# First feature block of two tiles ahead, x2 and x3 requested later, Gelu table preloaded: the start of a fused attention and GLU kernel

## The chip, the cores and the metric

The kernel runs on one core of a Trainium2 chip. The metric is the device time of one execution, in microseconds. Engines are called PE (matrix multiply), VectorE (DVE in the profile), ACT (ScalarE), POOL and SP, which issues the DMAs. Where this text says "trace", it means one profiled execution; a time is a median of several executions, unless said otherwise.

## The reference

```
xn = layernorm(x)                              # x: 1 x 2048 x 512, bf16
qkv = xn @ wqkv                                # 512 x 1536; 32 heads of 16
attention over 8 positions, 2 apart, its own the last;   s = attn @ wo
g = silu((gelu(xn @ w_gate) * (xn @ w_up)) @ w_down)    # inner width 1792
out = x + s * g
```

The 2048 rows are 16 tiles of 128, and four row blocks of 512. Feature blocks are the four groups of 128 of the 512 features; a matmul contracts over one of them.

## The kernel before

The start, cut to what the change touches. `x_sb[:, t]` is tile t; `wqkv_sb[:, k]` is weight block k. All DMAs are issued by SP in program order. The scheduler is off: each engine runs its instructions in the order written.

```python
    for i in range(2):
        for t in (2 * i, 2 * i + 1):
            load_x(t)
        for k in (2 * i, 2 * i + 1):
            nc.sync.dma_start(out=wqkv_sb[:, k, :], in_=A_wqkv[k * P : (k + 1) * P, :])
    load_x(TPQ, TPQ)                    # tiles 4 to 7; then w_gate, w_up, the rest of x
    ...
    first_stats(0); first_moments(0)    # VectorE statistics, then ACT square root
    first_stats(1); first_rstd(0); first_moments(1)
    normalize(0)                        # VectorE, 512 columns
    transpose(0)                        # four PE transposes, one ACT copy
    first_rstd(1); normalize(1)
    warm_up(4, P)
    transpose(1, parts=2, copy=nc.vector.tensor_copy)   # two copies
    for t in (2, 3): first_stats(t); first_moments(t)
    for t in (2, 3): first_rstd(t); normalize(t)
    for dk in range(NC):                # 4 blocks of 12 matmuls on tiles 0 and 1
        for n, (fo, ps) in enumerate(pairs):
            ...two matmuls 128 x 256...
            if dk == 2 and n in (2, 5):
                transpose(2 + (n == 5), copy=nc.vector.tensor_copy)
    ...
    for t in range(TPQ, 2 * TPQ): moments(t)            # statistics of tiles 4 to 7
    ...projections of tiles 2 and 3 ("second half"), then the GLU of row block 0...
```

The softmax here doesn't subtract the row's maximum and nothing guards it: scores larger than these inputs give would overflow.

## Time and profile before

| | kernel before |
|---|---|
| time, three executions | 229.1 us (229.09 to 229.49) |
| span of the trace | 227.4 us |
| PE busy | 98% |
| first matmul that counts | 6.55 us |
| second-half projections start | 12.45 us |
| second up-projection starts | 20.93 us |

PE sets the end. From 6.55 us to the tail it has almost no gap, so what matters is when PE starts and whether something then makes it wait. The three last rows are used as marks; they are starts in PE's timeline, which lists instructions by start and length. The profile's lines for this are in the prediction.

### The profile page before, as it was taken

How to read it: one execution, taken by the hardware profiler on the slowest of the kernel's cores; microseconds unless marked ns; L12 is line 12 of the kernel's file. 1: busy time of each engine (PE TensorE's matmuls, PEld its weight loads, DVE VectorE, ACT ScalarE, POOL GpSimd, SP SyncE). 2: the span in 40 equal slices, each digit the busy share in tenths (PEclk: the TensorE clock that was granted, in tenths of full speed). 3: DMA queues.
4: the chain of work that ended last, by engine and by line, in shares of the span. 5: the costliest groups of instructions: out<-in, count | busy, mean ns of one | idle time of the engine just before them, and what ended most of it. 6: DMA issues, size and time to landing. Idle time of an engine off the chain costs nothing.

```text
span 227.4 us, 3595 instructions
## 1 busy us (share of the span) xinstructions
PE 222.3 (98%) x1326; PEld 107.1 (47%) x1326; DVE 151.8 (67%) x278; ACT 132.2 (58%) x209; POOL 25.0 (11%) x67
## 2 busy tenths in 40 slices
PE   8999999999999999999999999999999999999993
PEld 4785444444444444444444444444444444444453
DVE  4696981899995588969904759924934348971434
ACT  4279769777531676766751466767763356756210
POOL 1027901000040000333700000000000000000000
PEclk9999999999999999999999999999999999999998
DMA  6999499941039911100219921100217950000011
GB/s 206 349 395 384 127 201 142 321 109 67 28 83 202 223 25 25 29 10 0 92 33 206 214 71 29 26 18 0 81 26 151 197 140 0 0 0 22 12 37 56
DMA packets 30130, 24.64 MB, mean 108 GB/s; under 512 B 10784, under 2 KB 29600, under 8 KB 30112
## 3 DMA queue, kind: packets, MB, share of 16 engines
q1 hardware_dynamic: 30112, 24.41, 44.3%
q8 instruction: 10, 0.16, 0.3%
q14 instruction: 8, 0.07, 0.1%
HBM read 18.74 MB, written 4.34 MB: 102 GB/s over the span
## 4 chain that ended last, share of the span: by engine, by line
PE 95%; DVE 1%; ACT 1%; DMA 1%; issue 0%; DVEq 0%
PE y_ps L443 21%; PE u_ps L249 21%; PE g_ps L249 21%; PE qkv_ps L249 16%; PE s_ps L459 6%; PE L_ps L338 3%; PE o_ps L406 3%; PE qk_ps L554 2%; DMA x_sb<-in_A_x_dram 1%; PE v_ps L554 1%; ACT L431 1%; DVE stats L182 1%; PE tr L214 1%; PE den_ps L358 0%; ACT ge L431 0%; ACT vst L273 0%
## 5 line engine op out<-in xcount | busy, mean ns | idle before, releaser
L249 PE MATMUL u_ps<-xnT,wu_sb 128*128 128x512 bf16 x224 | 57.5, 379 | 0.0
L249 PE MATMUL g_ps<-xnT,wg_sb 128*128 128x512 bf16 x224 | 57.5, 379 | 0.0
L443 PE MATMUL y_ps<-wd_sb,h 128*128 128x512 bf16 (+1 forms) x238 | 49.9, 367 | 0.0
L435 DVE TENSOR_TENSOR h<-ge,u 128x512 bf16<-128x512 bf16 x56 | 23.8, 425 | 30.7 <-ACT u L433 29.0
L433 ACT ACTIVATE u<-u_ps 128x512 bf16<-128x512 f32 x56 | 33.5, 598 | 16.4 <-PE u_ps L249 16.4
L431 ACT ACTIVATE ge<-g_ps 128x512 bf16<-128x512 f32 x56 | 33.5, 598 | 16.2 <-PE g_ps L249 16.0
L320 DVE TENSOR_TENSOR pk<-q_sb,k_sb 128x1024 bf16<-128x1024 bf16 (+1 forms) x56 | 38.9, 762 | 4.6 <-ACT k_sb L273 4.6
L392 DVE TENSOR_TENSOR pv<-E,v_arr 128x1024 bf16<-128x1024 bf16 (+1 forms) x48 | 39.8, 863 | 0.2 <-issue 0.2
L249 PE MATMUL qkv_ps<-xnT,wqkv_sb 128*128 128x512 bf16 (+1 forms) x192 | 37.0, 352 | 0.0
L443 PEld LDWEIGHTS <-h 128*128 128x128 bf16 x238 | 23.0, 98 | 25.9 <-issue 1.3
L249 PEld LDWEIGHTS <-wu_sb 128*128 128x128 bf16 x224 | 21.9, 98 | 26.6 <-issue 0.3
L249 PEld LDWEIGHTS <-wg_sb 128*128 128x128 bf16 x224 | 21.7, 98 | 26.3 <-issue 0.8
L451 ACT ACTIVATE sl<-y_ps 128x512 bf16<-128x512 f32 (+1 forms) x17 | 9.7, 572 | 32.6 <-PE y_ps L443 32.6
L249 PEld LDWEIGHTS <-wqkv_sb 128*128 128x128 bf16 x192 | 18.8, 98 | 17.5
L467 DVE TENSOR_TENSOR m<-s_ps,sl 128x512 bf16<-128x512 f32 (+1 forms) x17 | 11.1, 655 | 17.0 <-PE s_ps L459 17.0
L418 DVE TENSOR_TENSOR oT<-o_ps,rb 128x1024 bf16<-128x1024 f32 x8 | 9.4, 1220 | 13.8 <-DMA rb<-rs_d 13.8
L199 POOL TENSOR_TENSOR rstd<-rstd,mhalf 128x1 f32<-128x1 f32 x12 | 8.0, 663 | 69.9 <-DVE rstd L196 69.9
L459 PE MATMUL s_ps<-wo_sb,oT 128*128 128x512 bf16 (+1 forms) x68 | 14.8, 366 | 0.0
L273 ACT ACTIVATE vst<-qkv_ps 128x512 bf16<-128x512 f32 x14 | 8.4, 597 | 3.7 <-PE qkv_ps L249 3.7
L273 ACT ACTIVATE k_sb<-qkv_ps 128x512 bf16<-128x512 f32 x14 | 8.4, 601 | 3.2 <-PE qkv_ps L249 3.2
L273 ACT ACTIVATE q_sb<-qkv_ps 128x512 bf16<-128x512 f32 x14 | 8.3, 603 | 3.0 <-PE qkv_ps L249 3.0
L459 PEld LDWEIGHTS <-oT 128*128 128x128 bf16 x68 | 6.7, 98 | 7.2
(57 smaller groups left out, 131.4 us busy)
## 6 DMA issues: line engine op xcount, KB each, us to landing
v_arr<-vT SPq DMA_DIRECT2D x16, 520.0 KB, 8.5
vT<-vst SPq DMA_DIRECT2D x8, 256.0 KB, 2.2
out_dram<-o_t SPq DMA_DIRECT2D x15, 128.0 KB, 3.4
wg_sb<-in_B_w_gate_dram SPq DMA_DIRECT2D x2, 896.0 KB, 10.1
wu_sb<-in_B_w_up_dram SPq DMA_DIRECT2D x2, 896.0 KB, 11.0
wd_sb<-in_B_w_down_dram SPq DMA_DIRECT2D x1, 1792.0 KB, 11.5
wqkv_sb<-in_A_wqkv_dram SPq DMA_DIRECT2D x4, 384.0 KB, 4.9
x_sb<-in_A_x_dram SPq DMA_DIRECT2D x3, 512.0 KB, 10.5
```

The costliest lines, as they stand in the source:

```text
L249: nc.tensor.matmul(ps, lhsT=w[:, dk, lo : lo + P], rhs=xnT[j][:, dk, i0 : i0 + n], start=(dk == 0), stop=(dk == NC - 1),)
L273: nc.scalar.activation(out=dst, in_=ps, func=AF.Copy)
L320: nc.vector.tensor_tensor(out=st[j]["pk"][w][:, c0 : c0 + n, :], in0=st[j]["q"][:, c0 : c0 + n, :], in1=k_sb[j][:, c0 : c0 + n, off : off ...
L392: nc.vector.tensor_tensor(out=pv[:, d : d + n, :], in0=st[j]["E"][:, wh, :].unsqueeze(1).to_broadcast([P, n, TQ]), in1=st[j]["va"][:, 4 * ...
L418: nc.vector.tensor_tensor(out=oT[:, g : g + 2, :], in0=st[j]["o"][:, g : g + 2, :], in1=st[j]["rb"][:].unsqueeze(1).to_broadcast([P, 2, TQ ...
L431: nc.scalar.activation(out=ge[:], in_=g_ps[:], func=AF.Gelu_apprx_tanh)
L433: nc.scalar.activation(out=u[:], in_=u_ps[:], func=AF.Copy)
L435: nc.vector.tensor_tensor(out=h[:], in0=ge[:], in1=u[:], op=ALU.mult)
L443: nc.tensor.matmul(y[:], lhsT=st[j][fc][:, tt * P : (tt + 1) * P], rhs=wd_sb[:, fc, cols], start=(fc == 0), stop=(fc == NF - 1),)
L451: nc.scalar.activation(out=sl[:], in_=y[:], func=AF.Silu)
L459: nc.tensor.matmul(s[:], lhsT=st[j]["oT"][:, g, tt * P : (tt + 1) * P], rhs=wo_sb[:, g, cols], start=(g == 0), stop=(g == NC - 1),)
L467: nc.vector.tensor_tensor(out=m[:], in0=s[:], in1=sl[:], op=ALU.mult)
```

## The change

The intent: PE needs only the first feature block of tiles 0 and 1 to begin. So that block alone is normalized, transposed and copied first, and the other three follow behind the first six matmuls. Weight block 2, for which PE waited at 9.17, is requested ahead of x2 and x3. The Gelu table is loaded while ACT has nothing else to do.

```diff
-    for i in range(2):
-        for t in (2 * i, 2 * i + 1):
-            load_x(t)
-        for k in (2 * i, 2 * i + 1): ...
+    for t in (0, 1): load_x(t)
+    for k in range(NC - 1): load_wqkv(k)
+    for t in (2, 3): load_x(t)
+    load_wqkv(NC - 1)
... normalize() and transpose() take a list of feature blocks ...
-    normalize(0)
-    transpose(0)
+    normalize(0, [0])
+    transpose(0, [0])
+    warm_up(2, P)
     first_rstd(1)
-    normalize(1)
-    warm_up(4, P)
-    transpose(1, parts=2, copy=nc.vector.tensor_copy)
-    ...statistics and normalization of tiles 2 and 3...
+    normalize(1, [0])
+    transpose(1, [0])
+    normalize(0, rest)
+    normalize(1, rest)
     for dk in range(NC): ...
+            if dk == 0 and n == 2:
+                transpose(0, rest)
+                transpose(1, rest, nc.vector.tensor_copy)
+                for t in (2, 3): first_stats(t); first_moments(t)
+                nc.scalar.preload_act_table(AF.Gelu_apprx_tanh)
+                for t in (2, 3): first_rstd(t); normalize(t)
```

More of the change, by code (lines that the diff above doesn't have):

```diff
@@ L96, in load_w, with load_wqkv @@
         )
-    for i in range(2):
-        for t in (2 * i, 2 * i + 1):
-            load_x(t)
-        for k in (2 * i, 2 * i + 1):
-            nc.sync.dma_start(out=wqkv_sb[:, k, :], in_=A_wqkv[k * P : (k + 1) * P, :])
+    def load_wqkv(k):
+        nc.sync.dma_start(out=wqkv_sb[:, k, :], in_=A_wqkv[k * P : (k + 1) * P, :])
+    for t in (0, 1):
+        load_x(t)
+    for k in range(NC - 1):
+        load_wqkv(k)
+    for t in (2, 3):
+        load_x(t)
+    load_wqkv(NC - 1)
     load_x(TPQ, TPQ)
@@ L201, with normalize, transpose @@
     xns = {}
-    def normalize(t):
-        xn = xns[t] = xnp.tile([P, D], BF16, name="xn")
+    def normalize(t, cs=range(NC)):
+        if 0 in cs:
+            xns[t] = xnp.tile([P, D], BF16, name="xn")
+        cols = slice(cs[0] * P, (cs[-1] + 1) * P)
         nc.vector.tensor_scalar(
-            out=xn[:], in0=x_sb[:, t, :], scalar1=mv[:, t, 0:1], scalar2=rstd[:, t, :],
+            out=xns[t][:, cols], in0=x_sb[:, t, cols],
+            scalar1=mv[:, t, 0:1], scalar2=rstd[:, t, :],
             op0=ALU.subtract, op1=ALU.mult,
         )
-    def transpose(t, parts=1, copy=None):
-        xn = xns[t]
-        tr = mm.tile([P, NC * P], BF16, name="tr", tag="mm")
-        for c in range(NC):
-            nc.tensor.transpose(tr[:, c * P : (c + 1) * P], xn[:, c * P : (c + 1) * P], ident[:])
+    trs = {}
+    def transpose(t, cs=range(NC), copy=None):
+        if 0 in cs:
+            trs[t] = mm.tile([P, NC * P], BF16, name="tr", tag="mm")
+        tr = trs[t]
+        for c in cs:
+            nc.tensor.transpose(
+                tr[:, c * P : (c + 1) * P], xns[t][:, c * P : (c + 1) * P], ident[:]
+            )
         j, i = divmod(t, TPQ)
-        if i == 0:
+        if j not in xnT:
             xnT[j] = xtp.tile([P, NC, TQ], BF16, name="xnT")
-        dst = xnT[j][:, :, i * P : (i + 1) * P]
-        src = tr[:].rearrange("p (c n) -> p c n", c=NC)
-        for k in range(parts):
-            c = slice(k * NC // parts, (k + 1) * NC // parts)
-            if copy is None or k % 2:
-                nc.scalar.activation(out=dst[:, c], in_=src[:, c], func=AF.Copy)
-            else:
-                copy(out=dst[:, c], in_=src[:, c])
+        c = slice(cs[0], cs[-1] + 1)
+        dst = xnT[j][:, c, i * P : (i + 1) * P]
+        src = tr[:].rearrange("p (c n) -> p c n", c=NC)[:, c]
+        if copy is None:
+            nc.scalar.activation(out=dst, in_=src, func=AF.Copy)
+        else:
+            copy(out=dst, in_=src)
     def warm_up(n, cols):
@@ L533 @@
     warm_up(4, P)
+    rest = range(1, NC)
     first_stats(0)
@@ L538 @@
     first_moments(1)
-    normalize(0)
-    transpose(0)
+    normalize(0, [0])
+    transpose(0, [0])
+    warm_up(2, P)
     first_rstd(1)
-    normalize(1)
-    warm_up(4, P)
-    transpose(1, parts=2, copy=nc.vector.tensor_copy)
-    for t in (2, 3):
-        first_stats(t)
-        first_moments(t)
-    for t in (2, 3):
-        first_rstd(t)
-        normalize(t)
+    normalize(1, [0])
+    transpose(1, [0])
+    normalize(0, rest)
+    normalize(1, rest)
     for dk in range(NC):
@@ L560 @@
                 )
+            if dk == 0 and n == 2:
+                transpose(0, rest)
+                transpose(1, rest, nc.vector.tensor_copy)
+                for t in (2, 3):
+                    first_stats(t)
+                    first_moments(t)
+                nc.scalar.preload_act_table(AF.Gelu_apprx_tanh)
+                for t in (2, 3):
+                    first_rstd(t)
+                    normalize(t)
             if dk == 2 and n in (2, 5):
```

## The prediction

> **What bounds the kernel now.** I read the page first, for shares, then the chain that ended last, to see where TensorE stops being the end-setter.
>
> ```profile
> PE 222.3 (98%) x1326; PEld 107.1 (47%) x1326; DVE 151.8 (67%) x278; ACT 132.2 (58%) x209; POOL 25.0 (11%) x67
> ...
> PE 95%; DVE 1%; ACT 1%; DMA 1%; issue 0%; DVEq 0%
> ```
>
> PE is busy 98% of the span and is 95% of the chain, so outside PE's idle time only PE work can be saved. The edit touches only the start and one table load, so I followed the chain in order of time through the first 25 us.
>
> ```profile
> 0.80 2.12 DMA x_sb<-in_A_x_dram
> ...
> 5.69 0.40 PE tr L214 x4
> ...
> 6.12 0.30 DVE xnT L225
> 6.42 0.14 issue
> 6.55 0.60 PE v_ps L554 x4
> ...
> 17.89 0.60 ACT vst L273
> 18.48 0.49 ACT xnT L223
> ...
> 18.99 1.28 ACT L431
> ...
> 20.28 0.61 ACT ge L431
> ...
> 20.93 1.02 PE u_ps L249 x4
> ```
>
> Columns are start, length, what. Until 6.55 the chain is x's landing, statistics, normalization, transpose and copy; from 6.55 it is PE, with one detour through ACT at 17.89 to 20.93 which contains a table load of 1.28 us. The whole head that the edit can attack is thus what lies before 6.55, plus PE's small gaps. PE's gaps come from its timeline (start, length, engine, line, operation; consecutive equal ones merged):
>
> ```profile
> 7.86 0.60 PE L554 MATMUL v_ps<-xnT,wqkv_sb 128*128 128x256 bf16 x4
> 8.30 1.04 PE L554 MATMUL qk_ps<-xnT,wqkv_sb 128*128 128x256 bf16 x8
> 9.37 0.61 PE L554 MATMUL v_ps<-xnT,wqkv_sb 128*128 128x256 bf16 x4
> 9.81 0.38 PE L554 MATMUL qk_ps<-xnT,wqkv_sb 128*128 128x256 bf16 x2
> 10.03 0.39 PE L214 MATMUL tr<-ident,xn 128*128 128x128 bf16 x4
> 10.26 0.82 PE L554 MATMUL qk_ps<-xnT,wqkv_sb 128*128 128x256 bf16 x6
> ```
>
> A block dk of 12 matmuls takes 1.31 us (6.55 to 7.86). The second starts at 7.86, so the third was due at 9.17 and began at 9.37: 0.20 us is lost, and the waits name the landing of wqkv_sb block 2 (0.3 us on the weight-load row). Four transposes take 0.23 us of PE's time (10.03 to 10.26); the 0.39 is latency. The first up-projection ends at 19.64, four transposes bring PE to 19.86, the next gate projection to 20.72; the next up-projection starts at 20.93, so 0.21 us goes to the first Gelu, late by its table load. After 20.93 the timeline shows PE without gaps worth naming until the tail.
>
> **What the Trainium skill says.** "ScalarE: Activation LUTs", section "What ACT_TABLE_LOAD costs", gives about 1283 ns for a load, plus a drain; the trace has 1.28 us and no visible drain beside it. "ScalarE", section "Table sets: the hidden batching unit", says that cheap functions such as copy are in every set: so the copies between a preloaded Gelu table and the first Gelu force no reload, and the trace agrees (the copies at 12.64 to 18.97 run on the square-root table). "DMA: Bandwidth & Descriptors", section "Why a DMA increments its semaphore by 16 and not by 1", says that a transfer is complete only when every engine that carries a share has landed; the trace agrees in that landings lag the bytes (below). "TensorE: Matmul & The Clock Gate", Part 1, warns of a half clock after some 3.4 us idle; the longest PE gap after the change is under 1 us, and the granted clock here is 1.00 in every stretch of the head, so I give it nothing.
>
> **The change, part by part.**
>
> (1) Shorter head. Tile 1 sets it. Its reciprocal waits for its square root (4.68 to 4.97), not for tile 0's normalization, so its normalization still starts at 5.21. Cost of 128 columns instead of 512: tile 0 and 1 take 0.38 and 0.41; a one-column operation takes 0.15, so the slope is about 0.5 ns a column and 128 columns take some 0.21. That saves 0.20: the transpose starts at 5.48, not 5.69. One transpose (0.22 latency) instead of four (0.40) saves 0.18: end 5.71. The copy is now on ACT, for 128 columns: ACT takes 0.60 for 512 and 0.38 for 256, so 0.27 for 128, against VectorE's 0.29. End 6.02 (with 0.03 to start), and with the same 0.14 to the first matmul, 6.16. **Gain 0.4 us**.
>
> (2) Six transposes (three blocks of two tiles) are moved behind the first matmul of the bound, at 0.056 us each: **cost 0.33 us**. Their normalizations (384 columns, 0.35 each, 5.4 to 6.1) are done before PE gets there (6.16 plus half a block 0.65 is 6.81). Transposes end at 7.14, the copies at about 7.6, and PE's other half block ends at 7.80, so block 1 should not wait. Parts 1 and 2 nearly cancel.
>
> (3) Block 2 asked for before x2 and x3. **Gain 0.20**: the gap at 9.17 should go, since block 2 lands about 1 us earlier, and PE reaches it at 9.1.
>
> (4) The price of (3): x2 and x3 land later. The landing times of single issues in the trace of before (issue start plus time to landing):
>
> ```profile
> L88 SPq DMA_DIRECT2D x_sb<-in_A_x_dram x1: 432/432/432, 2.7 to 2.7; - x1
> DMA to landing us min/median/max: 4.0/4.0/4.0
> ...
> L88 SPq DMA_DIRECT2D x_sb<-in_A_x_dram x1: 432/432/432, 3.1 to 3.1; - x1
> DMA to landing us min/median/max: 5.0/5.0/5.0
> ...
> L103 SPq DMA_DIRECT2D wqkv_sb<-in_A_wqkv_dram x1: 432/432/432, 3.6 to 3.6; - x1
> DMA to landing us min/median/max: 5.7/5.7/5.7
> ```
>
> The first is x2 (landed 6.65), the second x3 (8.15), the third block 2 (9.3). Blocks 0 and 1 land at 5.3 and 6.3. 384 KB cost 1.0 to 1.15 us, 128 KB about 0.35, but x3 came 1.5 after x2: while it waited, the queues moved bytes at 328 GB/s, but one of the 16 shares lagged. If the lag stays where it is in time, block 2 lands at 8.5, x2 at 8.9, x3 at 9.3. If it belongs to the alternation of x and weights, block 2 lands at 7.35 and x2 at 7.7 to 8.0, x3 at 8.1 to 8.5. From x2's landing to tile 2's transpose I count two statistics (0.82 and 0.70 start to start), 0.27 to the normalization, 0.41 for it, 0.05: 2.25 us, as the order runs both tiles' statistics before either normalization. PE reaches tile 2's transpose at 6.16 + 1.31 + 0.33 + 1.31 + 0.65 = 9.76. With x2 at 7.9 it is ready at 10.15: PE **waits 0.4 us**; at 7.5 nothing; at 8.9, 1.4.
>
> (5) Gelu's table is loaded after the square root of tile 3, at 10 to 11, and ends before 12.6, where ACT next has work: **gain 0.21** at 20.72, no more, although the load is 1.28 us.
>
> Sum with x2 at 7.9: before, the second-half projections are reached at 12.61 on the chain; after, 10.15 + 0.23 + 0.65 + 0.23 + 1.31 = 12.57. So the head yields 0.04 and Gelu 0.21: **about 0.25 us, 229.1 to 228.9**.
>
> **Rivals.**
> A: x2 lands by 7.5. Then head plus block 2 give 12.61 - 12.18 = 0.43 and Gelu 0.21: 228.45. For it: 384 KB take 1.03 after block 1, and block 2 would land at 7.35; against it: x2 needs 0.35 more and a switch.
> B: the late transpose takes the place of both waits: x2 at 8.9 gives 10.15 + 1.0, so 1.0 lost against 0.25: 229.8. For it: before, the slot now given to x3 landed at 9.3.
> C: ACT's detour at 18 was not the table alone, and another buffer wait takes over at 20.72: 0.2 less gain. Against it: without the load Gelu ends near 19.6, 1.3 us before it is needed.
> D: a VectorE bound behind the head (its chain of statistics for tiles 4 to 7 feeds the transpose at 17.68, and its input is ready only about 0.3 earlier): the gain of the head would stop at 0.3. It only matters under A.
>
> **Range and chances.** A quarter for something like A, half near the middle, a quarter towards B. The three runs of before spread over 0.4 us. Predicted 228.9, range 228.4 to 229.6. All of it is within 0.5% of 229.1; 2% is 4.6 us, which is most of the head. So faster 0.01, same 0.98, slower 0.01.
>
> **What would show it.** The first v_ps matmul near 6.16; six transposes in block 0 adding 0.33; no wait for block 2; x2's landing, and with it whether PE's timeline has a gap before tile 2's transpose, its releaser being tile 2's normalization on VectorE; a table load near 10.5 and none near 19; no PE gap near 20.7. The prediction is wrong if x2's landing is far from 7.9, if ACT's copies delay block 1, or if PE gets gaps after 21 us that it had not.

## More of the kernel before

Later in the program, and not edited by the change, the tiles of row blocks 2 and 3 are transposed by DMA, 16 DMA transposes for each row block, issued at the start of the GLU of the row block before:

```python
        at(("glu", 1, 0), transpose_by_dma, 2 * TPQ + i)
        at(("glu", 2, 0), transpose_by_dma, 3 * TPQ + i)
```

## The result, and the profile after

The changed kernel took 229.24 us (median of 6, 228.90 to 229.54) against 229.09 (median of 6, 228.83 to 229.54). The ratio was 1.0004, with a 95% interval of 0.9989 to 1.0019: the same. A ratio here is the mean time of one kernel's fast runs over that of the other's of the same rounds, so it is not quite the ratio of the medians.

The time did not move, yet the trace shows nearly every step of the prediction. PE's timeline of the changed kernel (start, length, engine, line, operation, and in brackets the idle time before and what ended it):

```profile
6.14 0.60 PE L563 MATMUL v_ps<-xnT,wqkv_sb 128*128 128x256 bf16 x4 [0.37 <-ACT xnT L235]
6.57 0.38 PE L563 MATMUL qk_ps<-xnT,wqkv_sb 128*128 128x256 bf16 x2
6.79 0.50 PE L225 MATMUL tr<-ident,xn 128*128 128x128 bf16 x6
7.12 0.82 PE L563 MATMUL qk_ps<-xnT,wqkv_sb 128*128 128x256 bf16 x6
7.91 0.60 PE L563 MATMUL v_ps<-xnT,wqkv_sb 128*128 128x256 bf16 x4
...
9.65 0.38 PE L563 MATMUL qk_ps<-xnT,wqkv_sb 128*128 128x256 bf16 x2
10.00 0.40 PE L225 MATMUL tr<-ident,xn 128*128 128x128 bf16 x4
```

The first matmul is at 6.14 and not 6.55. Six transposes take 0.33 us (6.79 to 7.12). Six matmuls of 0.109 follow, which would end at 7.77; the next block starts at 7.91, so 0.14 us goes to a wait, for the copy of tile 1's other blocks by VectorE (7.40 to 7.76). Two matmuls from 9.65 end at 9.87, and tile 2's transpose starts at 10.00: 0.13 us of waiting for tile 2's normalization. The x2 request landed at 7.72 us, which is its issue at 3.14 plus 4.6:

```profile
L88 SPq DMA_DIRECT2D x_sb<-in_A_x_dram x1: 432/432/432, 3.1 to 3.1; - x1
DMA to landing us min/median/max: 4.6/4.6/4.6
```

ACT loads its table at 9.80, and the second up-projection starts without a gap (all engines' timeline of the changed kernel):

```profile
9.80 1.28 ACT L577 ACT_TABLE_LOAD   x1
...
18.95 0.60 ACT L443 ACTIVATE ge<-g_ps 128x512 bf16<-128x512 f32 x1
...
20.70 1.03 PE L261 MATMUL u_ps<-xnT,wu_sb 128*128 128x512 bf16 x4
```

At this point the changed kernel is 0.23 us ahead (20.70 against 20.93), and it stays so up to the projections of row block 3, which start at 152.00 against 152.23. Then it loses more than it had. The chain of work that ended last, for the changed kernel, first by engine and then in that stretch (start, length, what):

```profile
PE 83%; SPq 9%; DVE 3%; DMA 2%; issue 1%; ACT 1%; DVEq 0%; ACTq 0%
```

```profile
142.01 2.17 SPq L253
...
149.33 1.23 SPq L253
...
150.60 2.38 DMA xnT<-xn
152.99 0.04 issue
153.03 1.02 PE qkv_ps L261 x4
```

SP stands in the chain with 9%, where before it did not appear. These are the 16 DMA transposes of tiles 12 to 15, one behind another at some 1.27 us. The last landed at 152.99. PE's timeline there:

```profile
152.00 0.81 PE L261 MATMUL qkv_ps<-xnT,wqkv_sb 128*128 128x512 bf16 x3
...
153.03 2.32 PE L261 MATMUL qkv_ps<-xnT,wqkv_sb 128*128 128x512 bf16 x10 [0.22 <-DMA xnT<-xn]
```

Three matmuls at 0.216 apart make the fourth due at 152.65. It needs the last transposed block and starts at 153.03: 0.38 us lost. (The bracket says 0.22 because the end of a matmul is modelled later than the next can start.) In the trace of before the same block landed at 152.52 and was needed at 152.87, so it had 0.35 us to spare. From 0.23 ahead the changed kernel is thus 0.15 behind, and its span is longer by that: 227.53 against 227.37.

The trace of after has some 23 matmul records fewer than that of before, one about every 10.8 us, each leaving a false gap of 0.05 us. Start to start, such a place is exactly two matmuls (0.43 us), so I read them as lost records and not as waits.

### The profile page after: what moved, and what is told of

It reads as the page before. It is cut to its first block, busy times and chain, and to the rows that moved or that the text cites. A ratio compares the mean times of both kernels' runs of the same rounds, so it can differ in the third digit from the quotient of the medians.

```text
span 227.5 us, 3574 instructions
## 1 busy us (share of the span) xinstructions
PE 221.3 (97%) x1303; PEld 106.9 (47%) x1324; DVE 152.2 (67%) x280; ACT 132.8 (58%) x210; POOL 25.9 (11%) x67
## 4 chain that ended last, share of the span: by engine, by line
PE 83%; SPq 9%; DVE 3%; DMA 2%; issue 1%; ACT 1%; DVEq 0%; ACTq 0%
PE y_ps L455 21%; PE u_ps L261 16%; PE qkv_ps L261 16%; PE g_ps L261 15%; SPq L253 9%; PE s_ps L471 5%; PE L_ps L350 3%; PE o_ps L418 3%; PE qk_ps L563 2%; DVE m L479 1%; DMA xnT<-xn 1%; DMA x_sb<-in_A_x_dram 1%; PE v_ps L563 1%; PE tr L225 1%; DVE stats L187 1%
## 5 line engine op out<-in xcount | busy, mean ns | idle before, releaser
L261 PE MATMUL u_ps<-xnT,wu_sb 128*128 128x512 bf16 x219 | 56.9, 379 | 0.3
L261 PE MATMUL g_ps<-xnT,wg_sb 128*128 128x512 bf16 x219 | 56.7, 379 | 0.2
L455 PE MATMUL y_ps<-wd_sb,h 128*128 128x512 bf16 (+1 forms) x233 | 49.3, 366 | 0.2
## 6 DMA issues: line engine op xcount, KB each, us to landing
wu_sb<-in_B_w_up_dram SPq DMA_DIRECT2D x2, 896.0 KB, 10.8
```

What stands on the lines that cost most here:

```text
L261: nc.tensor.matmul(ps, lhsT=w[:, dk, lo : lo + P], rhs=xnT[j][:, dk, i0 : i0 + n], start=(dk == 0), stop=(dk == NC - 1),)
L455: nc.tensor.matmul(y[:], lhsT=st[j][fc][:, tt * P : (tt + 1) * P], rhs=wd_sb[:, fc, cols], start=(fc == 0), stop=(fc == NF - 1),)
```

## The experiments

There were three questions. Is the head's gain real in other executions? Does the DMA transpose take it back because of the change, or by chance? And what do the parts win alone? Twelve runs in three calls answered most of it. Each call had one chip (11, 9 and again 11) and shared its runs of the kernel before, so times of different calls are compared with care. The table has one trace of each kernel; "early" is the edit of the second experiment. "x2" and "block 2" are landings. "To end" is the span minus the start of the second up-projection.

| trace | x2 | block 2 | first matmul | second half | second up-proj. | to end |
|---|---|---|---|---|---|---|
| before | 6.64 | 9.32 | 6.55 | 12.45 | 20.93 | 206.44 |
| changed | 7.72 | 7.42 | 6.14 | 12.42 | 20.70 | 206.83 |
| changed again | 7.89 | 7.58 | 6.37 | 12.69 | 20.96 | 206.43 |
| changed, no preload | 8.40 | 7.57 | 6.16 | 13.10 | 21.59 | 206.61 |
| before, early (1st) | 6.44 | 9.21 | 6.54 | 12.34 | 20.82 | 206.50 |
| changed, early (1st) | 7.64 | 7.31 | 6.37 | 12.58 | 20.86 | 206.43 |
| before, early, preload (1st) | 6.88 | 8.55 | 6.58 | 12.27 | 20.55 | 206.42 |
| changed, early, old order | 6.39 | 8.99 | 6.07 | 12.27 | 20.55 | 206.43 |
| changed, early, late | 7.77 | 7.45 | 6.23 | 12.39 | 20.98 | 206.45 |
| the same, no warm-up | 7.84 | 7.54 | 6.19 | 12.36 | 20.94 | 206.43 |
| before, early (2nd) | 6.85 | 8.80 | 6.55 | 12.24 | 20.72 | 206.42 |
| changed, early (2nd) | 7.85 | 7.52 | 6.17 | 12.56 | 20.84 | 206.44 |
| before, early, preload (2nd) | 6.33 | 8.40 | 6.49 | 12.18 | 20.45 | 206.43 |
| combined | 8.28 | 7.96 | 6.23 | 12.39 | 20.67 | 206.43 |

The last column is the key. After the second up-projection every trace takes 206.42 to 206.50 us, except the two in which the last DMA transpose came late. So all differences between traces of more than 0.08 us lie in the first 21 us, or in that one wait.

### The changed kernel again

No edit.

> The changed kernel itself, for more executions and a second trace. Theory T (the head gain of about 0.23 us is real, and the last DMA transpose of tiles 12 to 15 can take it back before the fourth matmul of the projections of row block 3, as it did by 0.38 us in the first trace): the head repeats within 0.1 us (first v_ps matmul near 6.14, second up-projection near 20.70), and the wait at about 153 us varies between traces, from 0 to some 0.5. Rival R1 (the loss at 153 is a fixed consequence of the change): the same wait of 0.3 to 0.4 again. Time over before: T 0.998 to 1.001, R1 1.0005 or more.

Measured: 229.18 us (228.93 to 229.72; 6 executions), ratio 0.9992 (0.9973 to 1.0011). The means are 229.28 and, for the kernel before, 229.48: here the changed kernel is the faster one, within noise. The wait at 153 did not come: the last block landed at 152.67 and was due at 152.91. So the rival that the wait is a fixed consequence of the change falls. But the head did not repeat within 0.1 us as I had expected; it was 0.27 us later at the second half. That part of the theory was wrong: the first matmul was at 6.37, although tile 1's block was ready earlier. The lines of PE's timeline in this trace:

```profile
4.63 0.63 PE L243 MATMUL warm_ps<-const-bfloat16-1.0 128*128 128x128 bf16 x4
5.06 0.31 PE L225 MATMUL tr<-ident,xn 128*128 128x128 bf16 x1
5.32 0.37 PE L243 MATMUL warm_ps<-const-bfloat16-1.0 128*128 128x128 bf16 x2
5.74 0.26 PE L225 MATMUL tr<-ident,xn 128*128 128x128 bf16 x1
```

In the first trace the four warm-up matmuls took 0.45 and the two 0.27: PE was still slow here until past 5 us, and the two warm-ups ran to 5.69, after tile 1's transpose could have gone (its weights were loading at 5.63). The rest of the delay of the first matmul is x0, which landed 0.09 later. Then the first two matmuls started 0.16 us apart and not 0.11, as in no other trace; that cost a further 0.11, and why PE was slow there stays open.

### Earlier DMA transposes, in the kernel before

```diff
-        at(("glu", 1, 0), transpose_by_dma, 2 * TPQ + i)
+        at(("down", 0, 3), transpose_by_dma, 2 * TPQ + i)
-        at(("glu", 2, 0), transpose_by_dma, 3 * TPQ + i)
+        at(("down", 1, 3), transpose_by_dma, 3 * TPQ + i)
```

SP then issues them ahead of the four output stores of the block before. The output stores go out later; in the traces only the end of the program waits for them.

> The kernel before with one edit: the DMA transposes for row blocks 2 and 3 are issued ahead of the output stores of the block before, so that they land many us earlier. Theory T: the trace of before had 0.35 us of slack there, but its slower executions (229.5) had a wait; the median falls by 0 to 0.2 us and the spread shrinks to some 0.2 us. Rival R1 and R2 (the spread has nothing to do with those transposes): no change in spread or median, within 0.1.

Measured: 229.06 us; five of six executions within 229.03 to 229.11, one at 229.60. The kernel before had 228.87 to 230.40. Ratio 0.9987 (0.9969 to 1.0004). The last block landed at 144.87, some eight us before its use. The shrinking spread is what the theory expects, though a second call (below) had 228.84 to 229.33, so I do not call it shown that this wait makes the spread of the kernel before.

### The same edit, in the changed kernel

> The changed kernel with the same edit. Theory T: no PE wait at 153, so the whole head gain arrives: 0.2 to 0.3 us below the kernel before with the same edit, and 0.3 to 0.5 below the kernel before (228.6 to 228.8). Rival R2 (the head gain is taken back elsewhere, or is not in the unprofiled runs): equal to the kernel before with this edit within 0.1.

Measured: 229.18 us (228.97 to 229.46), ratio 0.9990 (0.9971 to 1.0009). The wait is gone from the trace, and yet the changed kernel was not faster than the kernel before with the same edit: the means are 229.19 and 229.15. My expectation was missed and the rival held. The head itself had no gain in this execution (second up-projection at 20.86 against 20.82). So the DMA transpose explains the first trace, but not why the time stood still.

### The changed kernel without the Gelu preload

The line with the preload is taken out.

> The changed kernel without the early load of the Gelu table. By the prediction's sum the head gives 0.04 to 0.05 and Gelu 0.21: so PE gets its gap of 0.2 back before the second up-projection, which starts near 20.91, and what is left of the gain at that point is 0.02 to 0.05 us. If the preload did nothing: it starts near 20.70 as in the changed kernel.

Measured: 229.45 us (229.20 to 230.05), ratio 1.0005 (0.9986 to 1.0024). From second half to second up-projection it took 8.49 us; with the preload it takes 8.27 to 8.28 in the traces of the changed head as it stands, and without it 8.48 in those of the kernel before. So the preload wins 0.21 us, in every trace where nothing else holds PE between the two marks. This trace also shows the weak point of the new order of requests. PE's timeline:

```profile
9.67 0.38 PE L563 MATMUL qk_ps<-xnT,wqkv_sb 128*128 128x256 bf16 x2
10.68 0.40 PE L225 MATMUL tr<-ident,xn 128*128 128x128 bf16 x4 [0.62 <-DVE xn L212]
```

The x2 request landed at 8.40, 0.7 us later than in the first trace, and tile 2's transpose, due at 9.89, waited until 10.68. That is 2.28 us after the landing, as in the first trace (10.00 - 7.72). The packed trace, the full record of a profile, has 16 counts of the request's semaphore, one for each share of the transfer: 15 had come by 7.87, and the last one came at 8.40. The last DMA transpose also came late (153.67, due at 153.53), hence the 206.61.

### The preload alone, in the kernel before with early transposes

```diff
         first_moments(t)
+    nc.scalar.preload_act_table(AF.Gelu_apprx_tanh)
     for t in (2, 3):
```

> The kernel before with early DMA transposes and only the Gelu preload of the change. Theory T (the preload is worth its 0.2 us, the new head is worth on average nothing or less): PE keeps its head (first v_ps matmul 6.55, tile 2's transpose near 10.0), the gap before the second up-projection is gone (it starts near 20.6 to 20.7), and the time is 0.15 to 0.25 us below the kernel before with early transposes (229.06 in the first call), so 228.8 to 228.95, with little spread. Rival (the preload's gain is lost later): equal to 229.06.

Measured: 229.04 us (228.71 to 229.09; 5 executions), ratio 0.9993 (0.9981 to 1.0005). The gap is gone and the mark is at 20.55, better than any trace of the changed kernel. Part of that was luck: block 2 landed at 8.55 and PE had no wait for it. In time the expected 228.8 to 228.95 was missed, and the gain is not clear of noise.

### The old order of requests, with the new head

```diff
-    for t in (0, 1): load_x(t)
-    for k in range(NC - 1): load_wqkv(k)
-    for t in (2, 3): load_x(t)
-    load_wqkv(NC - 1)
+    x0, x1, blocks 0 and 1, x2, x3, blocks 2 and 3, as in the kernel before
```

> The changed kernel with early DMA transposes and the old order of requests (x2 and x3 ahead of blocks 2 and 3). T: tile 2's transpose no longer waits for x2 but PE waits again for weight block 2, landing at 9.2 to 9.3, before the third block of matmuls, by 0 to 0.2 us (PE gets there at 9.1 to 9.4). Second up-projection at 20.6 to 20.75; time 0 to 0.2 us below the changed kernel with early transposes. Rival (x2's landing was not what held the head): tile 2's transpose again starts at 10.0 to 10.3 with a wait on VectorE's normalization.

Measured: 228.95 us (228.69 to 229.74), ratio 1.0000 (0.9985 to 1.0016). In the trace neither x2 nor block 2 made PE wait: PE reached block 2's matmuls at 9.14, and it had landed at 8.99. Tile 2's transpose, due at 9.80, went at 9.85. These 0.05 us are VectorE's: with x2 there at 6.39 it began tile 2's statistics only at 7.60, behind its copy of tile 1. The second half began at 12.27, against 12.58 and 12.56 in the two traces with the new order and early transposes. Against the second of them x2 explains 0.19 and an earlier x0 (2.81, not 2.92) the rest. The first had no wait for x2 either: its 0.06 before tile 2's transpose is VectorE's too (statistics at 7.91, x2 at 7.64), and it was late from the first matmul on. So the rival, that x2's landing was not what held the head, falls for one of the two traces and stands for the other. The executions spread over a full microsecond, I have no trace of a slow one, and their mean of 229.11 is that of the kernel before in this call (229.10).

### Tiles 2 and 3 transposed half a block later

```diff
-            if dk == 2 and n in (2, 5):
-                transpose(2 + (n == 5), copy=nc.vector.tensor_copy)
+            if (dk, n) in ((2, 5), (3, 2)):
+                transpose(dk, copy=nc.vector.tensor_copy)
```

> The changed kernel with early DMA transposes, and the transposes of tiles 2 and 3 half a block of matmuls later each. T: the wait for tile 2's normalization (0.03 to 0.6 us in the three traces) is gone unless x2 lands after 8.2: projections of the second half start at 12.15 to 12.4, the second up-projection at 20.4 to 20.7, and the median falls to 228.7 to 228.95. Rival (the head does not set the end any more): unchanged at 229.2.

Measured: 229.12 us; all five executions within 229.09 to 229.13, ratio 1.0000 (0.9988 to 1.0013). Tile 2's transpose no longer waited, and these five executions spread over 0.04 us. The median did not fall to the expected 228.7 to 228.95. In the trace another wait took the place:

```profile
16.32 1.47 PE L261 MATMUL qkv_ps<-xnT,wqkv_sb 128*128 128x256 bf16 x12
17.93 0.40 PE L225 MATMUL tr<-ident,xn 128*128 128x128 bf16 x4
18.16 1.03 PE L261 MATMUL g_ps<-xnT,wg_sb 128*128 128x512 bf16 x4
```

Twelve matmuls from 16.32 at 0.109 end at 17.63; the transpose of tile 4 starts at 17.93. VectorE's normalizations begin only at 17.47, because its copies and casts came later and the statistics of four tiles stood ahead of them. This is the bound D of the prediction, here met from the other side: its input moved later.

### The same, without the two warm-ups

```diff
     transpose(0, [0])
-    warm_up(2, P)
     first_rstd(1)
```

> As the run before it, without the two warm-up matmuls between the transposes of tiles 0 and 1. In two of four traces of the changed head those ran slowly (0.37 instead of 0.27 us, weight loads 0.15 instead of 0.10) and ended after tile 1's block was ready, so the first v_ps matmul was at 6.37 instead of 6.14. Theory W (they stand in the way): the first matmul at 6.14 to 6.2 in every trace, 0.1 us less on average. Rival (without them PE's clock comes up later): matmuls of the first block at twice the time, 0.3 us or more lost.

Measured: 229.08 us (228.93 to 229.13; 5 executions), ratio 0.9997 (0.9985 to 1.0009). From the landing of x0 to the first matmul the trace took 3.25 us. With the warm-ups that was 3.25 or 3.26 in four traces and 3.40 to 3.45 in three; without them it was 3.25 here and in the combined run. PE did not come up later. But this does not test warm-ups that stand in the way: in both traces without them the four warm-ups before had taken 0.39 and 0.40, so PE was already quick, as in the four quick traces (0.40 to 0.45). In the three slow ones they took 0.63, and no trace has that case without the two. The runs agree with theory W but do not show it.

### Both anchors again, the preload alone again, and all mends together

The third call put four kernels on one chip. The first is the kernel before with early transposes, the second the changed kernel with them.

> Anchor on this chip: the kernel before with early DMA transposes. 229.05 to 229.15, nearly all executions within 0.15 us of each other, second up-projection at 20.8 to 20.95.

> Anchor on this chip: the changed kernel with early DMA transposes. T (the new head's gain depends on the landing of x2 and on PE's slow start, execution by execution): median 229.0 to 229.3, spread 0.4 us or more, and thus equal to the anchor of before within 0.15 us. Rival (the first call fell in bad executions): 0.2 us below the anchor of before.

Measured: 228.95 us (228.84 to 229.33; mean 229.04) and 229.14 us (228.98 to 229.40; mean 229.15). Again the changed kernel is not the faster one: 0.04 and 0.11 us against it, within noise.

> The anchor of before plus the Gelu preload alone, now with both anchors on the same chip. T: 0.1 to 0.2 us below the anchor of before, and no slower than the changed kernel with early transposes: the preload is all that the change is sure to win.

Measured: 229.23 us (228.59 to 230.12; mean 229.26), ratio 1.0005 (0.9981 to 1.0029). The expectation was missed in time: the mean of the anchor of before was 229.04. The traced execution, at 228.59, was the shortest (block 2 at 8.40, mark at 20.45), and another took 230.12. The spread is open: no slow execution of this kernel was traced.

The last kernel takes the changed kernel with early transposes, the later transposes of tiles 2 and 3, no warm-ups, and this:

```diff
     for t in range(TPQ, 2 * TPQ):
         moments(t)
+        if t > TPQ:
+            normalize(t - 1)
```

with only tile 7's normalization left among the projections, moved from their fourth slot to the first.

> The changed kernel with early DMA transposes, tiles 2 and 3 transposed half a block later, no warm-up between the first two transposes, and VectorE normalizing tiles 4 to 6 between the statistics of tiles 5 to 7 and not after all of them. T (each of these waits held the head in turn; the last was VectorE's chain, 0.14 us before tile 4's transpose): no PE wait before tile 4's transpose, second up-projection at 20.4 to 20.65, median 228.6 to 228.8 with a spread under 0.2 us. Rival (something else holds the head at 20.9 to 21.0): 229.1 again.

Measured: 228.79 us (228.67 to 229.57; five of six within 228.67 to 228.84), ratio 0.9989 (0.9969 to 1.0009). PE's timeline around tile 4's transpose:

```profile
12.39 5.40 PE L261 MATMUL qkv_ps<-xnT,wqkv_sb 128*128 128x256 bf16 x48
17.63 0.39 PE L225 MATMUL tr<-ident,xn 128*128 128x128 bf16 x4
```

The second-half start is the same 12.39 as in the run that waited until 17.93; now the transpose goes at 17.63 without a wait, although x2 landed as late as 8.28. The second up-projection starts at 20.67 (20.65 at most was expected), so VectorE's order was worth 0.3 us. The median is in the expected range; one of the six took 229.57, so the spread is not under 0.2. It is the lowest median of that call (the kernel before had 228.98), but the interval holds 1, so it is not shown to be faster than the kernel before.

## Why the prediction was right or wrong

**Time and class.** 228.9 was forecast, 229.24 measured, inside 228.4 to 229.6, and "the same" was right. That is a weak test: the range is 1.2 us wide, and the six executions of either kernel spread over 0.64 and 0.71. The expected gain of 0.25 us did not come.

**Step 1, shorter head: right in mechanism, a little too sure.** From x0's landing the first matmul came 3.63 us later in the five traces of the old head. With the new one it came 3.25 to 3.45 later. The gain is 0.18 to 0.38, where 0.39 was forecast; the low values are those of the traces in which the warm-ups before were slow. That 6.14 came so near to 6.16 is in part luck: the normalization of 128 columns took 0.28, not 0.21, and the hop from the copy to the first matmul 0.05, not 0.14. The prediction gave PE's slow start nothing, as the granted clock was 1.00. That reading does not carry: from 2.90 to 4.60 in the second trace of the changed kernel the granted clock is 1.00 too, and there PE's 512-column matmuls on zeros start 0.43 us apart, where in another trace (the second of the changed kernel with early transposes) two of them start 0.22 apart.

**Step 2, six transposes: 0.33 us as forecast, but one term was missing.** "Block 1 should not wait" failed: VectorE's copy of tile 1 ends at 7.76, not 7.6, and block 1 waits 0.13 to 0.14 us in the traces. With that the parts 1 and 2 do more than cancel.

**Step 3, block 2: the gain of 0.20 was read off one trace.** It was the largest of the five traces of the old order with the old head. Block 2 landed at 9.32, 9.21, 8.80, 8.55 and 8.40, and PE wants it at 9.17. The wait was 0.20, 0.10 and three times nothing, on average 0.06 us. In the trace of before, 14 of the 16 shares of block 2 had landed by 7.91 and the last two at 9.19 and 9.32. So the wait hung on two late shares; for x3 the prediction had read one (15 by 6.97, the last at 8.17).

**Step 4, x2 late: right in mechanism.** 2.25 us from landing to transpose was forecast, and 2.28 to 2.29 measured in the three traces in which x2 set it. In the two others (x2 at 7.89 and 7.64) VectorE's copy of tile 1 ended after x2's landing and held the statistics; PE waited 0.06 there, a floor that the prediction did not have. Landing at 7.7 to 8.0 was forecast for the middle case; it came at 7.64 to 7.89 in four of the five traces of the new head (the preload taken out in one) and at 8.40 in the fifth. Rival B, with x2 at 8.9, was too dark, but its mechanism is what the trace with x2 at 8.40 shows.

**Step 5, Gelu: right.** 0.21 us was forecast; the stretch from second half to second up-projection shrank from 8.48 to 8.27 us. Rival C fell.

**What failed is the sum, before any run.** The 0.04 us for the head is 12.61 less 12.57, and these are two kinds of mark. 12.57 adds up starts of PE's instructions; 12.61 is read off the chain, which counts from the modelled end of a matmul. The start before was 12.45. By the prediction's own terms (0.39 - 0.33 + 0.20 - 0.39) the head loses 0.12 to 0.13, and with Gelu's 0.21 the change wins some 0.09 and not 0.25. Rival A has the same slip: 12.45 - 12.18 is 0.27, not 0.43. So it is luck that the first trace showed 0.23: x2 landed at 7.72, PE waited 0.13 where 0.39 was counted, and block 1's wait took back 0.14.

**And one trace is not the mean.** Take five traces of each head: for the new one the first two, the one without the preload, and the two with early transposes alone; for the old one the one of before and the four with early transposes. The second half began on average at 12.30 with the old head and at 12.67 with the new one. At the first matmul 0.30 us are won; then some 0.33 are paid for the six transposes, 0.14 for the copy and 0.26 before tile 2's transpose (0.06 of it the floor, the rest x2), with 0.06 won back at block 2. The preload's 0.21 covers only part of the 0.37. That leaves the changed kernel about 0.16 us behind in these traces; without the one trace with x2 at 8.40 it is 0.06. In time it is 0.04 and 0.11 behind with early transposes, and without these 0.09 behind in the first result and 0.20 ahead after it. None of it is clear of noise.

**What was not foreseen** is the last DMA transpose. The prediction had named a new gap after 21 us as a sign of being wrong, and this is one. "After 20.93 the timeline shows PE without gaps worth naming" was true, and it hid a chain with only 0.35 us to spare. In two of three traces with the changed head and late transposes it took 0.38 and 0.18 us. The third had no such wait, so the change does not force it. In all four traces with late transposes one issue in that chain was long (1.89 to 2.38 us) and overlapped a 16 KB fetch of instructions that occupied a DMA engine for 1.1 to 1.5 us, from 142.7 to 143.6 on. With the early edit no issue of this chain but the first took over 1.34. That this fetch causes the delay is argued from the coincidence, not shown.

**Open:** what the executions above 229.5 us do. They occur with the kernel before, with the changed one and in five of the eleven other versions; none but one, at 229.9, was traced, and that one had x2 and the DMA transpose late. In the first call they were 1 of 12 with early transposes and 11 of 23 without, but the other two calls do not repeat that (5 of 45 with, 1 of 22 without).

## What to carry to other kernels

A wait read off one trace is one draw when a landing ends it: look at how much that landing moves between traces before counting it as a gain. A request moved ahead pushes another one back, and the price is the length of the chain behind the one pushed back. When a gain is real at its place and missing at the end, subtract a mark behind the edit from the span: where the rest is constant, the cause is ahead of the mark, and where it is not, there is a second chain with little slack. And before a forecast subtracts two marks, both must be of one kind, both starts or both taken from the chain.

## What the Trainium skill lacked or had wrong

- "ScalarE: Activation LUTs", What ACT_TABLE_LOAD costs: a switch is put at some 2.66 us with its drain. Here the load took 1.28 us and Gelu followed 0.01 later; taking it off the path won 0.21 us, as the rest was beside PE's work.
- "TensorE: Matmul & The Clock Gate", Part 1: it tells that the start of full speed varies, and the runs agree (the same four warm-ups took 0.39 to 0.63 us). It has nothing on warm-ups placed between dependent steps. In the three of seven traces in which the warm-ups before were slow, the first matmul came up to 0.2 us later; that the two between the transposes cause this is not shown.
- "DMA: Bandwidth & Descriptors": Queues, rings and completion order does not say how much the landing of one and the same request moves between executions; the x2 request, issued at 3.14 us in all eight traces with the new order, landed at 7.64 to 8.40 us. And DMA Transpose (X-bar) gives no issue time for a single transpose from SBUF to SBUF; each of 128 x 128 held SP for some 1.23 us, so 16 of them make a chain of some 22 us to the last landing.
